# Odd rows of an eight-fold Fourier split: two residues in one tile, rows 376 apart summed and subtracted before the products

## The chip, the cores and the metric

The kernel runs on one core of a Trainium2 chip. A core has five engines with a queue each, which run their instructions in order and wait for one another through semaphores: TensorE (PE, matrix products; PEld is its weight load), VectorE (DVE), ScalarE (ACT), GpSimd (POOL) and SyncE (SP, which issues transfers). The metric is the device time of one execution in microseconds; all times here are in microseconds unless marked ns.

## The reference

```python
def _attn_ref(x):                      # x: (8, 3008, 256) float32
    X = np.fft.fft(x, axis=1)
    X = np.fft.fft(X, axis=2)
    return X.real.astype(np.float32)

def _moe_ref(x, w_in, w_out):          # x: (24064, 256), w_in: (256, 2048), w_out: (2048, 256)
    h = x @ w_in
    g = np.where(h > 0.0, h, 1.0 * (np.exp(np.minimum(h, 0.0)) - 1.0))
    return (g @ w_out).astype(np.float32)
```

The second function gets the result of the first, reshaped to 24064 rows of 256. So: a Fourier transform over 3008 rows and 256 channels for each of eight batches, real part, then two layers with an ELU between them.

## The kernel before, in words

**The main work.** The real part of the transform is symmetric, so half of the output rows (1504 a batch) give the rest. They are laid as columns, 256 to a tile, n_tiles = 47 tiles of 8 steps (376 steps). The transformed rows of a batch lie in two rings in SBUF (Rr for the cosine part, Ir for the sine part). One step i has, on PE, P (Wc times Rr, two products into a bank H), Q (Ws times Ir, two products added into the same bank), and for earlier steps seven products X1 (three), X2 (two) and X3 (two) into pA to pD. Between P and Q, DVE's E (even_part, L1263, two instructions) reads the bank, so Q waits for E. Then come h_minus (DVE, L1277), the ELU on ACT and DVE (g_plus and g_minus, L1293) and four sums and differences on POOL (sum_1, sum_3, sum_2, sum_4, in this order; L548), from which the seven products save an eighth. X1's third product reads what sum_2 writes, X2 what sum_3 and sum_1 write, X3 what sum_4 writes.

**How the order is set.** Every action is put into a list with a planned time, and the list is sorted and emitted; all that goes through `pin` keeps that order on its engine. A step is T = 4.8 long in the plan. Within a step: P at 0.0, E at 0.9, Q at 2.17, h_minus at 3.55; on POOL sum_4 of step i-2 at 0.3, then sum_1, sum_3, sum_2 of step i-1 at 2.91, 3.6 and 4.4. X1 of step i-2 stands at 0.87, behind P and ahead of Q; in the first step of a tile's eight X3 of the step before is moved behind P as well. At the end of a tile, in steps that are 1 modulo 8, comb_1 and comb_2 (two DVE instructions) stand at 4.2 and 4.21; comb_22 and comb_3 follow one step later at 1.0 and 2.5, the transposes turn_u and turn_v two and three steps later at 4.2, and each transpose is followed by SP's output transfers. Transfers of SP are not pinned, and run earlier than planned where they can.

**The transform.** Batches 2 to 7 (the Quarter class) split the 1504 half rows by eight. For the batch b, steps are counted from r0 = 48b - 70 by `rel`, so that r0 is 2 modulo 8:

- load_quarter (L276) brings four tiles j = 0 to 3 of x, first near rows (96 partitions) and then far rows (94 partitions); a partition holds four rows of 256, the residues m = 0 to 3 of a row number modulo 8. Two of the four (rows in rising order) come by SP (L301), two (falling order) by one indirect transfer each on POOL (L288). On POOL these are j = 1 in step 2, j = 2 in step 3 (5 for b = 2), j = 0 in step 27 and j = 3 in step 28, all at 1.3.
- mirror_sum (POOL), half_sum (DVE) and channel_fold (POOL) fold rows and channels into tiles e and o. quarter_pairs in steps 43 to 53 pairs them: for kodd = 0 on POOL, for kodd = 1 on DVE with multipliers of a table (L815, two instructions a call, at 4.25).
- at_quarter runs four transforms (ri = 0, 1 and kodd = 0, 1). Each has an even half and an odd half of four products into a bank H, in steps 51, 56, 59 and 64 and two steps later, at 4.75. The odd half (L963 to L967) has products of 189 or 188 columns: residues 1 and 3, u and v.
- DVE then spreads the halves, and join writes the rings: in steps 54, 59, 75 and 76.

A product in float32 shows in the trace as two PE passes with a weight load each, so counts of PE instructions are twice the counts of products.

The odd half before, and the place of the pairs for kodd = 1:

```python
            c, m = (378, 189) if self.kodd else (379, 188)
            yield (u, 1), c, 189, 0
            yield (u, 3), c + 189, 189, 0
            yield (v, 1), c + 378, m, 189
            yield (v, 3), c + 378 + m, m, 189
```
```python
        for n, step in enumerate((43, 44, 45, 46, 51, 53)):
            ri, m = divmod(n, 3)
            rel(step, 4.25, quarter_pairs, b, ri, 1, (2, 1, 3)[m])
```

Of the kernel before, what the change touches and what calls it, by code (L numbers as in the profile page):

```python
# [28 lines left out]
BE = 4 * NH  # L29
BW = BE + 3 * NE  # L30
NA = (95, 94)
QW = (1133, 1134)
GW = 7 * TW
PERIOD = 4.8
BS = 4
# [37 lines left out]
    return out.reshape(128, -1).astype(np.float32)  # L73


def _quarter_consts():

    p = np.arange(96)[:, None]

    def rows(m):  # L80
        s = 8 * p + m if m < 4 else 8 * (93 - p) + m
        return s, (p < (95 if m == 0 else 94)).astype(np.float64)

    out = []
    for ri in range(2):
        fn = np.cos if ri == 0 else np.sin
        for kodd in range(2):

            def block(m, k):
                s, w = rows(m)  # L90
                w = np.where(s == 0, 0.5, w)
                w = np.where(s == RUN, 0.5 if ri == kodd else 0.0, w)
                return w * fn(2.0 * np.pi * ((s * k[None, :]) % SEQ) / SEQ)

            def twist(m, n):
                s, w = rows(m)
                a = np.arange(n)[None, :]
                phi = np.pi * s / HALF
                turn = 2.0 * np.pi * ((2 * a * s) % HALF) / HALF
                c, d = np.cos(phi), np.sin(phi)  # L100
                if ri:
                    return w * d * np.cos(turn), w * c * np.sin(turn)
                return w * c * np.cos(turn), -w * d * np.sin(turn)

            n = 94 if kodd else 95
            near = 2 * np.arange(n) + kodd
            a, b = block(0, near), block(4, near)
            if kodd:
                (u1, v1), (u3, v3) = twist(1, 189), twist(3, 189)
                u2, v2 = twist(2, 95)  # L110
                parts = [a, u2, b, v2, u1, u3, v1, v3]
            else:
                ev, od = 4 * np.arange(189), 4 * np.arange(188) + 2
                parts = [a, b, block(2, ev[:95]), block(2, od[:94])]
                parts += [block(1, ev), block(3, ev), block(1, od), block(3, od)]
            out += parts
    return np.concatenate(out, axis=1).astype(np.float32)


def _turn_consts():  # L120
    p = np.arange(96)
    out = []
    for m in (1, 3, 2):
        t = np.tan(np.pi * np.minimum(8 * p + m, RUN - 1) / HALF)
        out += [t, -1.0 / t, 1.0 / t, -t]
    return np.stack(out, axis=1).astype(np.float32)


# [34 lines left out]
def kernel(  # L163
# [112 lines left out]
    def load_quarter(b, j, far):  # L276

        L = spool.tile([128, 6 * ND], FP, tag=f"xl{j}", bufs=1, name=f"xq{j}")
        if j == 0:
            state["rest"] = L[:, 4 * ND :]  # L280
        state["L", j, far] = L = L[:, 0 : 4 * ND]
        back = j in (1, 2)
        base = (0, SEQ, HALF, HALF)[j]
        if back != far:
            n = 94 if far else 96
            c = 3 if far else 5 if j == 1 and b == NB - 1 else 4
            pin(
                nc.gpsimd.indirect_dma_start(  # L288
                    out=L[0:n],
                    out_offset=None,  # L290
                    in_=xflat,
                    in_offset=bass.IndirectOffsetOnAxis(
                        ap=ix[0:n, c : c + 1].bitcast(U32), axis=0
                    ),
                    element_offset=(b * SEQ + (HALF if j in (1, 3) else 0)) * ND,
                )
            )
            return
        row = base - 751 if far else base
        for p, q in ((0, 80), (80, 94)) if far else ((0, 96),):  # L300
            nc.sync.dma_start(out=L[p:q], in_=xrows(b, row + 8 * p, 8, q - p, 4))  # L301

    CC = cpool.tile([128, 384], FP, tag="CC")
    w2 = cpool.tile([128, NF * ND], FP, tag="w2")
# [205 lines left out]
            out=t[0:96, 0 : QW[kodd]], in_=QM_dr.ap()[:, n : n + QW[kodd]]  # L510
        )

    twist_tab = cpool.tile([128, 12], FP, tag="turns")

    warm = cpool.tile([128, 1], FP, tag="warm")
    nc.vector.memset(warm, 0.0)
# [220 lines left out]
    def mirror_sum(j, far, m):  # L737

        n = 94 if far else 96
        own, other = lines(j, far)[0:n], lines((1, 2)[j == 3], far)[0:n, ::-1]  # L740
        gtt(own[:, m, 1:], own[:, m, 1:], other[:, m, :0:-1], ALU.add)
        if m == 0:
            gtt(own[:, :, 0:1], own[:, :, 0:1], other[:, :, 0:1], ALU.add)

    def half_sum(kodd, far, h):
# [32 lines left out]
    def quarter_row(b):  # L778

        L = state["L", 1, 0]  # L780
        if b == NB - 1:
            for i in range(3):
                act(L[0:1, i * ND : i * ND + ND], L[0:1, i * ND + ND : i * ND + 2 * ND])
        act(L[0:1, 3 * ND :], state["L", 0, 0][0:1, 0:ND])

    def quarter_pairs(b, ri, kodd, m):

        near, far = state["F", ri, kodd]
        slot = lambda m: (near, far)[m // 4][0:94, 128 * (m % 4) : 128 * (m % 4) + 128]
        parts = state.setdefault(("Q", ri, kodd, b), {0: near[0:95, 0:128], 4: slot(4)})  # L790
        if not kodd:
            if m == 1:
                state["pairs"] = spool.tile(
                    [128, 384], FP, tag="side", bufs=2, name="pairs"
                )
            new = state["pairs"]
            a, z = (
                t[0:94, 128:512].rearrange("p (m d) -> p m d", d=128)
                for t in (near, far)
            )  # L800
            o = new[0:94].rearrange("p (m d) -> p m d", d=128)
            if m == 1:
                gtt(o, a, z[:, ::-1], ALU.add)
            else:
                gtt(z[:, ::-1], a, z[:, ::-1], ALU.subtract)
            for k in (1, 2, 3):
                parts["u", k] = new[0:94, 128 * k - 128 : 128 * k]
                parts["v", k] = slot(8 - k)
            return
        new = (near, near, far)[m - 1][0:94, (512, 640, 512)[m - 1] :]  # L810
        parts["u", m], parts["v", m] = new[:, 0:128], slot(8 - m)
        for i, o in ((0, parts["u", m]), (1, parts["v", m])):
            c = 4 * (0, 2, 1)[m - 1] + 2 * ri + i
            pin(
                nc.vector.scalar_tensor_tensor(  # L815
                    out=o, in0=parts["v", m], scalar=twist_tab[0:94, c : c + 1],
                    in1=slot(m), op0=ALU.mult, op1=ALU.add,
                )
            )

    def fold_first(L):

# [125 lines left out]
    class Quarter(Dft):  # L948
        def parts(self, par):

            u, v = ("v", "u") if self.ri and not self.kodd else ("u", "v")
            if not par:
                order = (
                    ((0, 94), (("u", 2), 95), (4, 94), (("v", 2), 95))
                    if self.kodd
                    else ((0, 95), (4, 95), ((u, 2), 95), ((v, 2), 94))
                )
                c = o = 0
                for key, n in order:
                    yield key, c, n, o  # L960
                    c, o = c + n, o + n
                return
            c, m = (378, 189) if self.kodd else (379, 188)  # L963
            yield (u, 1), c, 189, 0
            yield (u, 3), c + 189, 189, 0
            yield (v, 1), c + 378, m, 189
            yield (v, 3), c + 378 + m, m, 189  # L967

        def mms(self, par, ps):
            parts = list(self.parts(par))  # L970
            for j, (key, c, n, o) in enumerate(parts):
                w = self.stat[key]
                K = w.shape[0]
                mm(
                    ps[:, o : o + n],
                    w,
                    QM[self.ri, self.kodd][0:K, c : c + n],
                    j == 0,
                    j == len(parts) - 1,
                )  # L980
            if par:
                self.odd = ps
            else:
                self.even = ps
# [932 lines left out]
    for b in range(2, NB):  # L1917
# [3 lines left out]
        def rel(step, dt, fn, *key):  # L1921
            at((r0 + step) * T + dt, lambda: fn(*key))
# [7 lines left out]
        rel(5, 3.0, quarter_row, b)  # L1930
        for far, start in ((0, 6), (1, 30)):
            for n in range(8):
                rel(start + n, 1.3, mirror_sum, (0, 3)[n % 2], far, n // 2)
        for step, *key in (
            (13, 0, 0, 0), (20, 1, 0, 0), (21, 0, 0, 1), (22, 1, 0, 1),
            (35, 0, 1, 0), (36, 1, 1, 0), (37, 1, 1, 1), (38, 0, 1, 1),
# [14 lines left out]
        for n, step in enumerate((43, 44, 45, 46, 51, 53)):  # L1951
            ri, m = divmod(n, 3)
            rel(step, 4.25, quarter_pairs, b, ri, 1, (2, 1, 3)[m])
        for step, ri, kodd, finish, join in (
            (51, 0, 0, 0, 54),
            (56, 1, 0, 0, 59),
            (59, 0, 1, 60, 75),
            (64, 1, 1, 66, 76),
        ):
            at_quarter(r0 + step, b, ri, kodd, r0 + finish, r0 + join)  # L1960
# [52 lines left out]
```

## Time and profile before

| | |
|---|---|
| median of 3 runs | 1916.73 us (1916.56 to 1917.5) |
| the profiled execution | 1918.8 us; its span, first to last instruction, 1917.0 |
| granted TensorE clock | 1.0 throughout |
| PE, DVE, ACT, POOL busy | 99%, 75%, 46%, 70% of the span |
| POOL sums (L548, G<-G) | 1440, 736 ns each |
| indirect loads (L288) | 24, 0.91 to 1.50 each |
| L815 pairs on DVE | 72, of 0.35 or 0.77 |
| loads by SP (L301) | 36 issues, 0.34 each in the median |
| SP waits for the transposed output (L1494 <- L1441) | 733.7 |

The page gives busy times and groups of instructions. A group's row has engine, operation, what it writes and reads, count, busy time, mean ns of one, and the idle time of the engine before it with what ended it. The timeline has one row for instructions of a kind that follow each other: start, length, engine, line, operation, operands and count; in brackets the idle time before it and what ended that. A row with x4 is four instructions. A wait is put down to the one that came last.

### The profile page before, as it was taken

What the parts mean: (1) busy time and instruction counts of PE and PEld (TensorE: products, weight loads), DVE (VectorE), ACT (ScalarE), POOL (GpSimd) and SP (SyncE); (2) the same over time, 40 slices, a digit from 0 to 9 for tenths busy, and PEclk for the clock granted to TensorE, in tenths of its full rate; (3) what the DMA queues carried; (4) which work ended last, traced back from release to release, by engine and by line L of the source; (5) the groups of instructions that cost most, each with busy time, mean ns of one, the idle gap of its engine ahead of it and who ended that gap; (6) DMA issues with size and microseconds to landing.
All of it is one profiled execution on the core that took longest, in us unless ns stands there. A gap on an engine that the chain in (4) does not pass through costs nothing.

```text
span 1917.0 us, 27564 instructions
## 1 busy us (share of the span) xinstructions
PE 1906.6 (99%) x8972; PEld 1656.8 (86%) x8972; DVE 1430.8 (75%) x2714; ACT 877.5 (46%) x1712; POOL 1348.7 (70%) x1837
## 2 busy tenths in 40 slices
PE   9999999999999999999999999999999999999999
PEld 6888888888888888888888888888888888888887
DVE  8766667877778777777777777777777777667666
ACT  5754444444444444444444444444444444344443
POOL 3888668776677766777667776687766876556565
PEclk9999999999999999999999999999999999999999
DMA  8146212111011110211101111022110210100101
GB/s 338 45 33 44 54 30 54 39 22 33 12 44 36 32 29 12 51 31 29 27 19 45 34 28 26 12 52 44 24 20 12 54 21 15 17 12 14 20 12 23
DMA packets 271072, 71.88 MB, mean 37 GB/s; under 512 B 256814, under 2 KB 257730, under 8 KB 270928
## 3 DMA queue, kind: packets, MB, share of 16 engines
q1 hardware_dynamic: 257296, 57.34, 15.1%
q0 software_dynamic: 11456, 12.52, 2.2%
q8 instruction: 71, 1.16, 0.2%
q14 instruction: 73, 0.60, 0.1%
q10 hardware_dynamic: 2176, 0.26, 0.1%
HBM read 45.20 MB, written 24.80 MB: 37 GB/s over the span
## 4 chain that ended last, share of the span: by engine, by line
PE 96%; DVE 2%; DMA 1%; ACT 1%; issue 0%; POOL 0%; SPq 0%; DVEq 0%; POOLq 0%
PE H L539 38%; PE pB L539 17%; PE pC L539 17%; PE pD L539 17%; PE pA L539 9%; DMA raw<-in_moe_w_in_dram 0%; DVE e L636 0%; DVE pow L407 0%; DVE E L1263 0%; POOL w L548 0%; DVE o L636 0%; ACT Wsc L551 0%; ACT G L551 0%; ACT M L551 0%; DMA wex<-wx 0%
## 5 line engine op out<-in xcount | busy, mean ns | idle before, releaser
L548 POOL TENSOR_TENSOR G<-G 128x256 f32<-128x256 f32 x1440 | 1046.2, 736 | 513.3 <-DVE G L1293 353.1
L551 ACT ACTIVATE G<-H 128x512 f32<-128x512 f32 x376 | 224.5, 597 | 930.9 <-DVE G L1277 927.2
L1263 DVE SCALAR_TENSOR_TENSOR E<-Rb,wex,H 128x256 f32<-128x256 f32 x752 | 328.1, 478 | 374.4 <-PE H L539 367.6
L539 PE MATMUL H<-Ir,Wsc 128*128 128x256 f32 x1504 | 386.7, 380 | 1.4 <-DVE E L1263 1.4
L539 PE MATMUL H<-Rr,Wsc 128*128 128x256 f32 x1504 | 387.3, 380 | 0.5 <-ACT Wsc L551 0.5
L539 PE MATMUL pC<-G,WT 128*128 128x256 f32 x1440 | 369.5, 379 | 0.0
L539 PEld LDWEIGHTS H<-Ir,Wsc 128*128 128x128 f32 x1504 | 278.4, 189 | 49.2 <-DVE E L1263 3.8
L539 PEld LDWEIGHTS H<-Rr,Wsc 128*128 128x128 f32 x1504 | 282.5, 190 | 41.7 <-issue 2.3
L539 PEld LDWEIGHTS pC<-G,WT 128*128 128x128 f32 x1440 | 273.6, 190 | 37.2
L1277 DVE SCALAR_TENSOR_TENSOR G<-E,H 128x512 f32<-128x512 f32 x376 | 257.2, 684 | 46.6 <-POOL G L548 13.2
L1293 DVE SCALAR_TENSOR_TENSOR G<-G,H 128x512 f32<-128x512 f32 x376 | 256.1, 681 | 40.7 <-ACT G L551 40.6
L1293 DVE SCALAR_TENSOR_TENSOR G<-M,G 128x512 f32<-128x512 f32 x376 | 257.1, 684 | 0.7 <-ACT M L551 0.7
L551 ACT ACTIVATE G<-G 128x512 f32<-128x512 f32 x376 | 233.4, 621 | 0.0
L539 PE MATMUL pB<-G,w 128*128 128x256 f32 x784 | 229.3, 379 | 0.0
L539 PE MATMUL pA<-G,w 128*128 128x256 f32 x784 | 229.3, 379 | 0.0
L539 PE MATMUL pD<-G,w 128*128 128x256 f32 x784 | 229.3, 379 | 0.0
L551 ACT ACTIVATE M<-G 128x512 f32<-128x512 f32 x376 | 224.3, 596 | 2.8 <-DVE G L1277 2.8
L551 ACT ACTIVATE M<-M 128x512 f32<-128x512 f32 x376 | 221.1, 588 | 0.1
L539 PE MATMUL pB<-G,WT 128*128 128x256 f32 x720 | 214.3, 379 | 0.0
L539 PE MATMUL pD<-G,WT 128*128 128x256 f32 x720 | 214.1, 379 | 0.0
L539 PEld LDWEIGHTS pA<-G,w 128*128 128x128 f32 x784 | 148.9, 190 | 20.5
L539 PEld LDWEIGHTS pB<-G,w 128*128 128x128 f32 x784 | 148.9, 190 | 20.4 <-PE H L539 0.2
(170 smaller groups left out, 1529.8 us busy)
## 6 DMA issues: line engine op xcount, KB each, us to landing
out_dram<-ot SPq DMA_DIRECT2D x496, 32.0 KB
xq<-in_x_dram SPq DMA_DIRECT2D x12, 384.0 KB
out_dram<-ot SPq DMA_DIRECT2D x256, 2.0 KB
xq<-in_x_dram SPq DMA_DIRECT2D x12, 320.0 KB
Rb<-r SPq DMA_DIRECT2D x10, 376.0 KB
raw<-in_moe_w_in_dram SPq DMA_DIRECT2D x7, 512.0 KB
MC<-dft_mats SPq DMA_DIRECT2D x3, 943.5 KB
xl<-in_x_dram SPq DMA_DIRECT2D x4, 512.0 KB
```

What stands on the lines that cost most here:

```text
L539: nc.tensor.matmul(out_, lhsT=lhsT, rhs=rhs, start=start, stop=stop, skip_group_check=True)
L548: pin(nc.gpsimd.tensor_tensor(out=o, in0=a, in1=b, op=op))
L551: pin(nc.scalar.activation(out=o, in_=i, func=func, **kw))
L1263: nc.vector.scalar_tensor_tensor(out=S.E[:, c], in0=Rb[:, cols(i)], scalar=wex[:, f : f + 1], in1=S.H[:, c], op0=ALU.mult, op1=ALU.add,)
L1277: nc.vector.scalar_tensor_tensor(out=two(S.G[:, 0:512])[:, :, ::-1], in0=two(S.E), scalar=2.0, in1=two(S.H), op0=ALU.mult, op1=ALU.subtract,)
L1293: nc.vector.scalar_tensor_tensor(out=o, in0=e, scalar=-1.0, in1=h, op0=ALU.add, op1=ALU.max)
```

## The change

Residues 1 and 3 of the odd rows are no longer held side by side. Rows 376 apart (SHIFT = 8 x 47) are put into two tiles at the same partition: 47 partitions with rows 8p + 3, 47 with rows 8p + 1, and the rows 376 higher in the other place. After the pairs, a new function shift_pairs forms the sum and the difference of the two; the sum goes with the even wave numbers and the difference with the odd ones, so each product has half the columns, written to every second column of the bank. For kodd = 1 this holds for all four products of the odd half, for kodd = 0 for two of four. It takes other load patterns, other constants and another order of the mirror sums. The diff, cut to what the text speaks of:

```diff
-QW = (1133, 1134)
+QW = (944, 756)
+NP = 47
+SHIFT = 8 * NP
...
         if back != far:
             n = 94 if far else 96
-            c = 3 if far else 5 if j == 1 and b == NB - 1 else 4
-            pin(
-                nc.gpsimd.indirect_dma_start(
-                    out=L[0:n],
...
+            for i in (0, 2) if far else (3, 1):
+                c = 3 if far else 5 if j == 1 and b == NB - 1 and i == 3 else 4
+                pin(
+                    nc.gpsimd.indirect_dma_start(
+                        out=rows[0:n, i],
...
+            row = base + (749 if far else -3)
+            for i, shift in (((3, 0), (1, SHIFT)) if far else ((2, 0), (0, SHIFT))):
+                nc.sync.dma_start(
+                    out=rows[0 : 2 * NP, i],
...
+                        ap=[[2 * ND, 2], [-8 * ND, NP], [1, ND]],
...
+            if not far:
+                nc.sync.dma_start(
+                    out=rows[2 * NP : 96, 0::2][:, 0:2],
...
             return
-        row = base - 751 if far else base
-        for p, q in ((0, 80), (80, 94)) if far else ((0, 96),):
-            nc.sync.dma_start(out=L[p:q], in_=xrows(b, row + 8 * p, 8, q - p, 4))
+
+        def ahead(p, n, first, row, step):
+            nc.sync.dma_start(
+                out=rows[p : p + n, first::2][:, 0:2],
...
+        for p, n in ((0, 80), (80, 14)) if far else ((0, 96),):
+            ahead(p, n, int(far), base + 8 * p - 750 * far, 2)
+        for p, m, n in ((0, 3, NP), (NP, 1, NP if far else 96 - NP)):
+            ahead(p, n, int(not far), base + m - 752 * far, SHIFT)
...
-        if m == 0:
+        if m == 1:
             gtt(own[:, :, 0:1], own[:, :, 0:1], other[:, :, 0:1], ALU.add)
...
         L = state["L", 1, 0]
-        if b == NB - 1:
-            for i in range(3):
-                act(L[0:1, i * ND : i * ND + ND], L[0:1, i * ND + ND : i * ND + 2 * ND])
...
-        parts["u", m], parts["v", m] = new[:, 0:128], slot(8 - m)
+        parts["u", m], parts["v", m] = new[:, 0:128], slot(1 if m == 1 else 8 - m)
         for i, o in ((0, parts["u", m]), (1, parts["v", m])):
...
+            turn(o, slot(8 - m), 4 * (0, 2, 1)[m - 1] + 2 * ri + i, slot(m), ALU.add)
+
+    def turn(o, a, c, b, op):
+
+        pin(
+            nc.vector.scalar_tensor_tensor(
+                out=o, in0=a, scalar=twist_tab[0:94, c : c + 1],
+                in1=b, op0=ALU.mult, op1=op,
+            )
+        )
+
+    def shift_pairs(b, ri, kodd, k):
+
+        near = state["F", ri, kodd][0][0:94]
+        parts = state["Q", ri, kodd, b]
+        m = "uv".index(k)
+        low, high = parts[k, 1], parts[k, 3]
+        sign = ALU.add, ALU.subtract
+        if kodd:
+            new = near[:, (384, 256)[m] :][:, 0:128], low
+            for o, f in zip(new, sign):
+                turn(o, high, 12 + (ri != m), low, f)
+        else:
+            new = near[:, 128:256], near[:, 384:512]
+            for o, f in zip(new, sign):
+                vtt(o, low, high, f)
+        for i in range(2):
+            parts[k, "+-"[i]] = new[i]
...
-            c, m = (378, 189) if self.kodd else (379, 188)
-            yield (u, 1), c, 189, 0
-            yield (u, 3), c + 189, 189, 0
-            yield (v, 1), c + 378, m, 189
-            yield (v, 3), c + 378 + m, m, 189
+            c = 378 if self.kodd else 379
+            for k, o in ((u, 0), (v, 189)) if self.kodd else ((u, 0),):
+                yield (k, "+"), c, 95, slice(o, o + 189, 2)
+                yield (k, "-"), c + 95, 94, slice(o + 1, o + 188, 2)
+                c += 189
+            if not self.kodd:
+                yield (v, 1), c, 188, slice(189, 377)
+                yield (v, 3), c + 188, 188, slice(189, 377)
...
-                rel(start + n, 1.3, mirror_sum, (0, 3)[n % 2], far, n // 2)
+                rel(start + n, 1.3, mirror_sum, (0, 3)[n % 2], far, (0, 2, 1, 3)[n // 2])
...
             rel(step, 4.25, quarter_pairs, b, ri, 1, (2, 1, 3)[m])
+        for step, *key in (
+            (47, 0, 1, "u"), (48, 0, 0, "u"), (49, 0, 1, "v"), (50, 1, 0, "v"),
+            (54, 1, 1, "u"), (55, 1, 1, "v"),
+        ):
+            rel(step, 4.25, shift_pairs, b, *key)
```

## The prediction

> **What bounds the kernel now.** I read the page first, then the timeline of TensorE (PE), VectorE (DVE) and GpSimd (POOL) around one batch (b=3), then the waits. Steps are counted from r0 of the batch, as in the code: E of step 27 starts at 552.90, of step 47 at 647.89, of step 54 at 683.31. On the page PE is busy for the whole span, and the chain that ended last lies on PE for 96%:
>
> ```profile
> PE 1906.6 (99%) x8972; PEld 1656.8 (86%) x8972; DVE 1430.8 (75%) x2714; ACT 877.5 (46%) x1712; POOL 1348.7 (70%) x1837
> ```
>
> So PE is the bound, at a period of 4.75 us a step (11 products of 256 columns, 0.43 each), and two things count: columns taken from PE, and any stall put into it. The averages of DVE and POOL say that there is room; the timeline says where there is none.
>
> **What PE saves.** The timeline of PE, at an even half (four products of 94 or 95 columns) and an odd half (four of 188 or 189) of one transform:
>
> ```profile
> 670.57 0.36 PE L539 MATMUL H<-QM,e 95*128 95x95 f32 x2
> 670.76 0.39 PE L539 MATMUL H<-QM,o 94*128 94x95 f32 x2
> 670.99 0.39 PE L539 MATMUL H<-QM,pairs 94*128 94x95 f32 x2
> 671.21 0.39 PE L539 MATMUL H<-QM,o 94*128 94x94 f32 x2
> 671.43 1.06 PE L539 MATMUL H<-Rr,Wsc 128*128 128x256 f32 x4
> ...
> 680.96 0.81 PE L539 MATMUL H<-QM,pairs 94*128 94x189 f32 x4
> 681.60 0.80 PE L539 MATMUL H<-QM,o 94*128 94x188 f32 x4
> 682.25 1.03 PE L539 MATMUL H<-Rr,Wsc 128*128 128x256 f32 x4
> ```
>
> From start to start a 95-column product takes 0.22 (670.76 to 670.99; two passes), a 189-column one 0.32 ((682.25 - 680.96)/4). Halving the columns saves 0.10, not half. With kodd=1 all four products of the odd half shrink (1.29 to 0.88, saves 0.41), with kodd=0 two (saves 0.20). Two of each a batch: 1.23 us; six batches: **-7.4**. The outputs are now written with a step of two columns, which no row shows. From one side: no cost, as 95 columns need 0.16 at the full rate (95 x 0.43/256) of the 0.22; from the other, a half-rate write would make 95 columns as long as 189, and the saving goes (0), or doubles the 0.22 (+2.6 a batch at worst). I take no cost: the nearest row is the contiguous 95-column one.
>
> **What DVE adds.** shift_pairs is 12 instructions a batch (six calls of two), 94x128 with both inputs in SBUF. The nearest row is L815, same shape, same place in a step; DVE and POOL beside each other:
>
> ```profile
> 631.72 0.35 DVE L815 SCALAR_TENSOR_TENSOR e<-o,twist_tab,e 94x128 f32<-94x128 f32 x1
> 632.10 0.77 DVE L815 SCALAR_TENSOR_TENSOR o<-o,twist_tab,e 94x128 f32<-94x128 f32 x1
> ```
> ```profile
> 631.20 0.72 POOL L548 TENSOR_TENSOR G<-G 128x256 f32<-128x256 f32 x1
> 632.00 0.73 POOL L548 TENSOR_TENSOR G<-G 128x256 f32<-128x256 f32 x1
> ```
>
> Each ends 0.15 after the POOL instruction that was running when it started (631.92 to 632.07, 632.73 to 632.87). So a pair lasts until the second POOL boundary after its start, plus 0.15. Now the six places. A call stands at 4.25 of its step, behind h_minus and, in steps 47 and 55, behind comb_1 and comb_2 too (47 + r0 is 1 modulo 8, where those stand at 4.2). Step 47, and the E of step 48 behind it:
>
> ```profile
> 651.06 0.68 DVE L545 TENSOR_TENSOR u<-p,pB 128x512 f32<-128x512 f32 x1
> 651.84 0.69 DVE L545 TENSOR_TENSOR v<-u,pC 128x512 f32<-128x512 f32 x1
> 652.64 0.87 DVE L1263 SCALAR_TENSOR_TENSOR E<-Rb,wex,H 128x256 f32<-128x256 f32 x2
> ```
> ```profile
> 652.39 0.73 POOL L548 TENSOR_TENSOR G<-G 128x256 f32<-128x256 f32 x1
> 653.08 0.99 POOL L548 TENSOR_TENSOR pairs<-e,o 94x384 f32<-94x384 f32 x1
> ```
>
> Behind E waits PE's Q: its weight load starts at 653.57, 0.06 after E's end (653.51), and in most steps the weight load of H<-Ir shows the same 0.07 of waiting for E. In step 29, where E came 0.10 late, PE lost about 0.03. So the cushion is 0.07 and the rest is paid one to one.
> - Step 47: first of the pair starts about 652.5, ends 653.12 + 0.15; second ends 654.07 + 0.15 = 654.22. E starts 0.08 before that (instructions overlap so), at 654.14 instead of 652.64: PE loses 1.50 - 0.07 = **1.43**.
> - Step 48: no loss by a hair. E of 49 has PE's X3 and X1 ahead of Q (Q at 658.48, E's end at 657.40, 1.08 spare), and the new pair brings it about 0.9 late. Steps 49 and 50 (turn_u, turn_v): E had 1.2 idle before it, the pair takes about 1.1: nothing. A margin missed costs 0.1 to 0.3 each.
> - Step 54: pair starts 687.0; POOL boundaries at 687.44 and 688.25, so it ends 688.40; E at 688.32 instead of 688.06: **0.18**.
> - Step 55: as 47. Pair from 692.61, POOL boundaries 693.29 and 693.97, end 694.12; E at 694.04 instead of 692.81, both sides 0.18 later: **1.16**.
>
> Sum 2.77 a batch, six batches: **+16.6**. If POOL did not hold it up a pair would take 0.7 (2 x 0.35), E would be 0.55 late at 47 and 55, and the sum is 2 x 0.48 x 6 = 5.8: the lower bound. Missed margins make 3.5 a batch, 21, the upper.
>
> **What POOL adds.** Each of the four indirect loads a batch becomes two. In steps 27 and 28 (j=0 and j=3, 94 rows):
>
> ```profile
> 552.97 1.49 POOL L288 DMA_INDIRECT xq<-in_x_dram,ix  x1 [0.18 <-issue]
> 554.52 3.46 POOL L548 TENSOR_TENSOR G<-G 128x256 f32<-128x256 f32 x4
> 558.16 1.49 POOL L288 DMA_INDIRECT xq<-in_x_dram,ix  x1 [0.18 <-issue]
> 559.68 3.48 POOL L548 TENSOR_TENSOR G<-G 128x256 f32<-128x256 f32 x4
> ```
>
> POOL has no idle time there: sums, load, sums. The load stands ahead of sum_1, and PE's third X1 product (pB<-G,WT) needs sum_2, the third of the four. In step 28 sum_2 ends at 562.06 and that weight load starts at 562.84: 0.78 spare. Two more loads at 1.49 + 0.18 push it 3.34 later: PE loses 2.56, 0.46 in step 28's X1 and the rest one step on. The sums there are stretched by DVE's join (0.88 and 1.03 instead of 0.73), and partly slide out of it: I take 2.3. Six batches: **+13.8**. The new loads have a quarter of the bytes per row, which no row shows at 94 rows; from the one side, the 96-row loads of steps 2 and 3 take 0.92 + 0.15, and with that price PE would lose about 0.1 a batch (0.6 in all); from the other, the loads that open the program stand 0.3 apart, 1.80 each: 2.8 a batch, 17. The first eight indirect loads (L239) have rows of 4 KB and 2 KB in turn and take 0.94 to 1.24 with no order by size, so I keep 1.49.
>
> [...]
>
> In steps 2 and 3 (96 rows) POOL idles 0.68 and 0.65 before its sums, so two times 1.07 leave it 0.8 late, against 1.5 of spare before X1: nothing; without that cover 2.1 a batch.
>
> **Costed at nothing.** SP issues 24 loads a batch instead of 6 (L301: 36 in all), 18 x 0.34 = 6 us, under 734 us in which SP waits for the transposed output; were that cover gone, stores would hold the two output tiles and DVE's transposes. The reordered mirror sums only swap rows; half_sum(35) now follows its last mirror sum in the same step, with some 2 us between (0.9 a batch if not). ACT loses three 0.4 us copies in the last batch, ACT is at 46%. Landing of the 94-row loads takes 11 to 12 us (96 rows 4.0); their first reader comes 14 us after: covered, and the pieces are smaller.
>
> **Sum.** -7.4 + 16.6 + 13.8 = +23.0. The profiled execution took 1918.8 (span 1917.0 and 1.8 around it), so a profiled one would take 1941.8; the median of the runs shown is 1916.7, 2.1 below, so **1939.7**.
>
> **Rivals.**
> - Faster: the added DVE and POOL work falls into idle time (25% and 30% on average). -7.4 gives 1909. It decides if the stalls stay under 1.23 us a batch; the only place that could do it is E of steps 48 and 56, and there DVE has 0.1 idle. 0.07.
> - Same, within 0.2% (3.8 us, about what a measurement of this kernel can tell from no change): pairs at 0.7 and POOL at the 96-row price: -7.4 + 5.8 + 0.6 = 1916. 0.06.
> - POOL's price is by bytes, only DVE stalls: -7.4 + 16.6 + 0.6 = 1926.5. For it: quarter rows; against: L239. 0.15.
> - DVE's pair escapes POOL, only POOL stalls: -7.4 + 5.8 + 13.8 = 1929. Against: every L815 pair. 0.07.
> - The change does not do what it says (stepped outputs eat PE's saving) or the hair margins of steps 48 to 50 break: +3 to +12 more, 1943 to 1952. 0.12.
> - The forecast, 1931 to 1946: 0.53.
>
> **Chances and range.** Faster 0.07, same 0.06, slower 0.87. The range leaves out the first two rivals and little above: 1922 to 1950.
>
> **What would show it.** Weight loads H<-Ir waiting for DVE E about 1.4, 0.2 and 1.2 in steps 48, 55, 56 of each batch; weight loads pB<-G,WT waiting for POOL G 0.5 and 1.8 in steps 28 and 29; 48 indirect loads with a mean near 1.2; odd halves of 0.88 and 1.09 from first product to the next P; PE busy down by some 7 and idle by some 30. The prediction is wrong if PE shows no such gaps, if a 94-row quarter load takes 0.9, or if 95-column products with stepped outputs stand more than 0.22 apart.

## The result, and the profile after

The changed kernel took 1942.25 us in the median of four runs (1941.26, 1941.78, 1942.72 and, profiled, 1948.1), the kernel before 1916.69 on the same chip: ratio 1.0139, 95% interval 1.0118 to 1.0159. It is slower by 25.6, where +23.0 was forecast. The profiled execution is 6 above the others; the prediction has nothing for that, and why is part of what follows.

The page of the changed kernel, its busy times and the chain that ended last (lines of the helpers have moved: matmul L587, POOL's sums L596, E L1332):

```profile
PE 1909.4 (98%) x8972; PEld 1649.0 (85%) x8972; DVE 1468.0 (75%) x2786; ACT 876.5 (45%) x1709; POOL 1380.8 (71%) x1861
...
PE 86%; DVE 5%; POOL 4%; DMA 2%; issue 1%; SPq 1%; ACT 0%; DVEq 0%; POOLq 0%
```

PE runs as many instructions as before, and is busy for 1909.4 instead of 1906.6. Its share of the chain fell from 96% to 86%: DVE, POOL, DMA and SP's queue now hold pieces of it. The waits of the changed kernel (who waits, for whom, us in total, times, longest) say where:

```profile
PEld H L587 <- DVE E L1332: 21.2, 24, 1.6
...
PEld pB L587 <- POOL G L596: 16.8, 15, 1.9
...
POOL xs L596 <- DMA xs<-xe_dr: 7.5, 1, 7.5
PEld H L587 <- POOL xe L596: 5.7, 1, 5.7
```

Before, the first was 3.8 in 7 waits and the second 0.6 in 2; the other two were not there. So there are three kinds of stall. I take the size of each from PE's own starts: the time from one pass to the next, less the 0.22 of a pass without a wait.

**Kind 1, E behind a pair.** DVE, POOL and PE at steps 47 and 48 of b=3 (start, length, operation, count, idle before it):

```profile
664.63 1.82 DVE L863 SCALAR_TENSOR_TENSOR e<-o,twist_tab,e 94x128 f32<-94x128 f32 x2
666.38 0.86 DVE L1332 SCALAR_TENSOR_TENSOR E<-Rb,wex,H 128x256 f32<-128x256 f32 x2
```
```profile
664.58 0.73 POOL L596 TENSOR_TENSOR G<-G 128x256 f32<-128x256 f32 x1
665.27 1.04 POOL L596 TENSOR_TENSOR pairs<-e,o 94x384 f32<-94x384 f32 x1
```
```profile
667.29 1.13 PE L587 MATMUL H<-Ir,Wsc 128*128 128x256 f32 x4 [1.21 <-DVE E L1332]
```

The pair ends at 666.45, 0.14 after POOL's second instruction (666.31), and E comes after it. PE's starts lose 1.47 to 1.48 here in every batch, 0.19 to 0.32 at step 55 and 0.88 to 1.02 at step 56 (0.67 in the last batch).

**Kind 2, X1 behind the loads.** POOL and the weight loads in step 28 of the same batch:

```profile
569.57 1.49 POOL L303 DMA_INDIRECT xq<-in_x_dram,ix  x1 [0.18 <-DVE G L1362]
571.37 1.50 POOL L303 DMA_INDIRECT xq<-in_x_dram,ix  x1 [0.30 <-issue]
572.89 5.20 POOL L596 TENSOR_TENSOR G<-G 128x256 f32<-128x256 f32 x7
```
```profile
568.63 0.30 PEld L587 LDWEIGHTS pB<-G,WT 128*128 128x128 f32 x2 [0.71 <-POOL G L596]
```

A quarter of the bytes, and still 1.49 for each load; the second has 0.30 of idle before it, where 0.18 stands before the first. PE loses 0.50 to 0.72 in step 28 and 1.76 to 1.78 a step later.

**Kind 3, once, at 198 us.** SP and POOL of the changed kernel, where the short rows (xs, one channel of all batches) are loaded:

```profile
188.78 0.30 SPq L1180 DMA_DIRECT2D xe_dr<-x  x1
189.12 0.70 SPq L337 DMA_DIRECT2D xq<-in_x_dram  x2
190.42 0.39 SPq L1186 DMA_DIRECT2D xs<-xe_dr  x1
190.85 2.91 SPq L1190 DMA_DIRECT2D xs<-xe_dr  x1
193.80 3.73 SPq L337 DMA_DIRECT2D xq<-in_x_dram  x4
```
```profile
197.16 0.39 POOL L596 TENSOR_TENSOR xs<-xs 128x96 f32<-128x96 f32 x1 [7.47 <-DMA xs<-xe_dr]
```

Before, SP issued the last of these xs loads at 182.56 and POOL went on at 189.4. Now five of batch 2's near loads (L317, L326, L337) stand ahead of the last xs load in SP's order, where one stood. Their issues take 2.7 in all, the one took 0.35. The last xs load is issued at 190.85, POOL waits 7.47, and PE loses 5.44. The other 6 of the 8.3 lie in SP's issues and waits that were there before and took longer in this execution, such as 9.68 instead of 7.42 for the four loads of x at 170.82.

The wait costs more than its length. These are the short rows' products behind it, in the changed kernel and in the kernel before, and the row of the changed kernel for the stretch 197.71 to 201.11 (its length, the busy times of PE, PEld, DVE, ACT and POOL, then the granted clock):

```profile
197.96 3.74 PE L587 MATMUL H<-MC,xe 128*8 128x189 f32 x24 [5.28 <-POOL xe L596]
```
```profile
193.60 2.09 PE L539 MATMUL H<-MC,xe 128*8 128x189 f32 x24
```
```profile
197.71:201.11 3.40, 3.15 (x23) 1.55 (x24) 0.00 (x0) 0.00 (x0) 3.24 (x7) 0.50 0.39 107
```

The granted clock is 0.50 there, and the same 24 passes take 1.65 more. So kind 3 costs 5.44 + 1.65 = 7.1.

**PE's saving.** The odd halves of the transforms, PE of the changed kernel, first kodd = 0, then kodd = 1:

```profile
694.68 0.58 PE L587 MATMUL H<-QM,e 94*128 94x95 f32 x4
695.10 0.83 PE L587 MATMUL H<-QM,o 94*128 94x188 f32 x4
695.77 1.03 PE L587 MATMUL H<-Rr,Wsc 128*128 128x256 f32 x4
...
737.85 1.03 PE L587 MATMUL H<-QM,e 94*128 94x95 f32 x8
738.71 1.06 PE L587 MATMUL H<-Rr,Wsc 128*128 128x256 f32 x4
```

From the first product to the next P: 1.09 and 0.86, both 1.29 before. Eight passes in 0.86 are 0.108 each, 0.215 a product: the stepped output costs nothing.

So the sum of this execution is -7.4 + 30.3 (5.0 a batch) + 7.1 = +30.0 by the predicted saving, and 1948.1 - 1918.8 = 29.3 by the two profiled executions. The 0.7 between them lies at the start: PE's first pass of P stands at 27.81 in the profile after and at 28.48 in the one before. In the profiles of the runs below it stands at 25.81 to 26.70, so both of these executions also began late, by 1.5 and 2.1 against a middle of 26.3.

### The profile page after: what moved, and what is told of

Read it like the earlier page. It is cut to its first block, busy times and chain, and to the rows that moved or that the text cites. A ratio compares the mean times of both kernels' runs of the same rounds, so it can differ in the third digit from the quotient of the medians.

```text
span 1946.3 us, 27882 instructions
## 1 busy us (share of the span) xinstructions
PE 1909.4 (98%) x8972; PEld 1649.0 (85%) x8972; DVE 1468.0 (75%) x2786; ACT 876.5 (45%) x1709; POOL 1380.8 (71%) x1861
## 3 DMA queue, kind: packets, MB, share of 16 engines
q8 instruction: 71, 1.16, 0.3%
## 4 chain that ended last, share of the span: by engine, by line
PE 86%; DVE 5%; POOL 4%; DMA 2%; issue 1%; SPq 1%; ACT 0%; DVEq 0%; POOLq 0%
PE H L587 34%; PE pB L587 15%; PE pC L587 15%; PE pD L587 15%; PE pA L587 8%; POOL G L596 2%; DMA x<-in_x_dram 2%; POOL xq L303 2%; DVE e L863 1%; DVE E L1332 1%; DVE v L593 1%; DVE G L1362 1%; DVE G L1346 0%; DVE u L593 0%; SPq L1162 0%
## 5 line engine op out<-in xcount | busy, mean ns | idle before, releaser
L596 POOL TENSOR_TENSOR G<-G 128x256 f32<-128x256 f32 x1440 | 1047.8, 737 | 497.5 <-DVE G L1362 344.0
L1332 DVE SCALAR_TENSOR_TENSOR E<-Rb,wex,H 128x256 f32<-128x256 f32 x752 | 327.4, 476 | 356.6 <-PE H L587 351.6
L587 PE MATMUL H<-Ir,Wsc 128*128 128x256 f32 x1504 | 388.8, 381 | 12.3 <-DVE E L1332 12.2
L587 PE MATMUL H<-Rr,Wsc 128*128 128x256 f32 x1504 | 387.6, 380 | 0.5 <-ACT Wsc L599 0.5
L587 PE MATMUL pC<-G,WT 128*128 128x256 f32 x1440 | 369.6, 379 | 0.0
L587 PEld LDWEIGHTS H<-Ir,Wsc 128*128 128x128 f32 x1504 | 277.8, 189 | 65.2 <-DVE E L1332 21.2
L587 PEld LDWEIGHTS H<-Rr,Wsc 128*128 128x128 f32 x1504 | 282.1, 190 | 41.8 <-issue 1.7
L587 PEld LDWEIGHTS pC<-G,WT 128*128 128x128 f32 x1440 | 273.6, 190 | 37.2
L1346 DVE SCALAR_TENSOR_TENSOR G<-E,H 128x512 f32<-128x512 f32 x376 | 257.0, 683 | 58.6 <-POOL G L596 24.6
L587 PE MATMUL pB<-G,w 128*128 128x256 f32 x784 | 229.3, 379 | 0.0
L587 PE MATMUL pA<-G,w 128*128 128x256 f32 x784 | 229.3, 379 | 0.0
L587 PE MATMUL pD<-G,w 128*128 128x256 f32 x784 | 229.3, 379 | 0.0
L587 PE MATMUL pB<-G,WT 128*128 128x256 f32 x720 | 215.7, 381 | 11.2 <-POOL G L596 11.2
L599 ACT ACTIVATE M<-G 128x512 f32<-128x512 f32 x376 | 223.9, 596 | 2.8 <-DVE G L1346 2.8
L587 PE MATMUL pD<-G,WT 128*128 128x256 f32 x720 | 214.2, 379 | 0.0
L587 PEld LDWEIGHTS pA<-G,w 128*128 128x128 f32 x784 | 149.0, 190 | 20.5
L587 PEld LDWEIGHTS pB<-G,w 128*128 128x128 f32 x784 | 148.9, 190 | 20.4 <-PE H L587 0.2
```

Source lines behind the costliest of these rows:

```text
L587: nc.tensor.matmul(out_, lhsT=lhsT, rhs=rhs, start=start, stop=stop, skip_group_check=True)
L596: pin(nc.gpsimd.tensor_tensor(out=o, in0=a, in1=b, op=op))
L599: pin(nc.scalar.activation(out=o, in_=i, func=func, **kw))
L1332: nc.vector.scalar_tensor_tensor(out=S.E[:, c], in0=Rb[:, cols(i)], scalar=wex[:, f : f + 1], in1=S.H[:, c], op0=ALU.mult, op1=ALU.add,)
L1346: nc.vector.scalar_tensor_tensor(out=two(S.G[:, 0:512])[:, :, ::-1], in0=two(S.E), scalar=2.0, in1=two(S.H), op0=ALU.mult, op1=ALU.subtract,)
```

## The experiments

The theory: three kinds of stall, each with its own cause, take back more than PE saves, and the saving itself is whole. Rivals: POOL's price goes by bytes; the stepped outputs cost PE time; the spread between runs has nothing to do with SP's order. Numbers of the runs are those of their labels (run 8, an earlier form of run 10, gave no result). The kernel before was timed beside each group of runs: 1916.6 to 1916.8.

### 1. The loads alone

The kernel before, with each indirect load of a row of four cut into two halves of 2 KB:

```diff
+            for h in range(2):
-                    out=L[0:n],
+                        out=L[0:n, 2 * ND * h : 2 * ND * h + 2 * ND],
-                    element_offset=(b * SEQ + (HALF if j in (1, 3) else 0)) * ND,
+                            b * SEQ + (HALF if j in (1, 3) else 0) + 2 * h
```

> The kernel before, each of its 24 indirect loads cut into two of half the columns (2 KB a row), all else unchanged. Theory: an indirect load costs POOL a fixed 1.5 us (94 rows) or 0.9 (96 rows) and 0.3 ahead of it, whatever its bytes, so PE waits for sum_2 in steps 28 and 29 of each batch, about 2.4 us a batch: +14.5, about 1931, with weight loads pB<-G,WT waiting for POOL. Rival, price by bytes: each half takes about half, no wait, 1917.

Measured 1930.65 (1930.34 to 1931.33), ratio 1.0067 (1.0044 to 1.009): +14.1. PE lost 0.49 to 0.72 and 1.76 to 1.78 a batch at X1, and nothing at E. The loads took 1.49 to 1.50 with half the bytes of a row, as with the whole row before and a quarter of it after. So the price does not go by bytes, and kind 2 comes from the number of loads alone.

### 2. The pairs alone

The kernel before, with the same 72 DVE instructions in the same places, of the same shape, written to columns that nothing reads; the products stay as they were:

```diff
+        for step, *key in (
+            (47, 0, 1, "u"), (48, 0, 0, "u"), (49, 0, 1, "v"), (50, 1, 0, "v"),
+            (54, 1, 1, "u"), (55, 1, 1, "v"),
+        ):
+            rel(step, 4.25, shift_pairs, b, *key)
```

> The kernel before with the 72 instructions of shift_pairs at their places, same operands and sizes, their results written to columns that nothing reads (one constant column for the multiplier); products and loads as before. Theory: E of steps 48, 55 and 56 comes late and PE's Q waits 1.5, 0.1 to 0.2 and 1.0 a batch: +15.8, about 1932.5. Rival, the pairs escape POOL or fit into idle time (0.35 each): +5.8 or less, at most 1922.5. Rival, that they only delay because POOL is late from its loads: 1917.

Measured 1932.18 (1932.04 to 1932.29), ratio 1.0075 (1.0051 to 1.0098): +15.6, with 1.46 to 1.48, 0.19 to 0.33 and 0.67 to 1.01 a batch. Kinds 1 and 2 add up: 14.1 + 15.6 - 7.4 = +22.3. The changed kernel's fastest run is at +24.6, so something over 2 is missing even there.

### 3. The pairs elsewhere

The changed kernel, the pairs at other steps and mostly ahead of h_minus (3.5 in a step) instead of behind it:

```diff
-            (47, 0, 1, "u"), (48, 0, 0, "u"), (49, 0, 1, "v"), (50, 1, 0, "v"),
-            (54, 1, 1, "u"), (55, 1, 1, "v"),
+            (48, 3.5, 0, 1, "u"), (49, 3.5, 0, 0, "u"), (50, 3.5, 0, 1, "v"),
+            (51, 4.26, 1, 0, "v"), (53, 4.26, 1, 1, "u"), (56, 3.5, 1, 1, "v"),
```

> The changed kernel with the six calls of shift_pairs at other places: ahead of h_minus in steps 48, 49, 50 and 56, behind h_minus in steps 51 and 53, where E has over 1 us of idle time ahead of it. Theory: the waits of Q for E go nearly all (2.6 a batch), POOL's stay: 15 below the changed kernel, about 1927. Rival, the DVE work is too much wherever it stands: no change, 1942.

Measured 1928.68 (1926.24 to 1930.85), ratio 1.006 (1.004 to 1.008). Kind 2 stayed as it was. At E 0.26 a batch was left, in step 50, where the pair of step 49 and the transpose turn_u stand in one step, and single stalls of 0.98 in two batches. Kind 3 cost nothing in this profile, with the same order on SP: the last xs load was issued at 182.7. So most of kind 1 is a matter of place.

### 4. 96 rows instead of 94

The changed kernel, far loads of 96 rows with the row numbers shifted so that all stay inside the batch; nothing reads the two added rows:

```diff
-            (3, 128, 748),
+            (3, 128, 764),
-            n = 94 if far else 96
+            n = 96
-                            b * SEQ + (HALF if j in (1, 3) else 0) + i
+                            b * SEQ + (HALF if j in (1, 3) else 0) + i - 16 * far
```

> The changed kernel, its 24 indirect far loads with 96 rows instead of 94 (two more rows of x into partitions that nothing reads). Theory: what makes a load cost POOL 1.5 instead of 0.9 is the 94 rows, so the loads take 0.92, step 28 has no wait and step 29 at most 0.5: 12 to 14 below the changed kernel, about 1929. Rival, the 1.5 comes from the place (DVE beside it) or the far rows' addresses: still 1.5, 1942.

Measured 1935.94 (1930.82, 1933.12, 1938.76, 1940.41), ratio 1.0102 (1.0073 to 1.0131), so the gain was there, but less than expected and with a wide spread. POOL in step 28 of b=3, in the profile of the 1930.82 run:

```profile
558.46 0.92 POOL L303 DMA_INDIRECT xq<-in_x_dram,ix  x1
559.68 0.92 POOL L303 DMA_INDIRECT xq<-in_x_dram,ix  x1 [0.30 <-issue]
560.62 5.70 POOL L596 TENSOR_TENSOR G<-G 128x256 f32<-128x256 f32 x7
```

More rows, and 0.92 instead of 1.49. The stall at X1 fell from 2.3 or 2.5 to between 0.6 and 1.1 in five batches and 1.6 in the last. It did not go, because two loads of 0.92 with 0.15 and 0.30 of idle take 2.3 of a step, where the one load of before took 1.67. This profile has no stall of kind 3 either (last xs load at 180.9), and the other three executions, up to 1940.41, have no profile.

### 5. Both together

> The changed kernel with the edits of the third and the fourth run together. The terms add: 1916.6 of before, -7.4 of shorter products, 3.9 of stalls at E that the third run kept (0.26 in each batch and two or three single ones), 5 of stalls behind the sums that the fourth run kept (0.6 to 1.1 a batch): 1918, plus a stall of 0 to 6 before step 26 where POOL waits for the last loads of the short rows. Rival, the two kinds of stall hide each other (a late sum gives DVE a boundary less): under 1914. Rival, a term was left out that the fourth run's median of 1935.9 showed: over 1926 in the median with no front stall in the profile.

Measured 1921.61 (1919.34 to 1925.59), ratio 1.0024 (1.0015 to 1.0034); the profiled execution was the one of 1919.34 and has no stall of kind 3. What it lost to the batches' stalls, some 9.5, gives 1916.7 - 7.4 + 9.5 = 1918.8: the terms add in that execution, and neither rival holds. The median lies 2.3 above it; no profile shows why.

### 6. The xs loads first

The changed kernel; `pin` holds an engine's instructions in the planned order, here for the xs loads and batch 2's near loads on SP:

```diff
+    def first_pin(b):
+        return pin if b == 2 else lambda i: i
...
-                nc.sync.dma_start(
+                first_pin(b)(nc.sync.dma_start(
                     out=rows[0 : 2 * NP, i],
...
-                nc.sync.dma_start(
+                pin(nc.sync.dma_start(
                     out=xs[:, j, :, 0:4],
```

> The changed kernel, with the last loads of the short rows (xs) and the near loads of batch 2 kept in the planned order on SP, so that the new loads come behind them. Theory, the new SP loads of batch 2 stand between those loads and make POOL's fold late, by an amount that differs from run to run: the last xs load is issued by 183, POOL's fold waits under 2, PE has no gap over 0.5 before the stall at step 28 of batch 2, and all runs lie within 1.5 of one another at 1938.5 to 1940.5 (1916.6 - 7.4 + 30.3 = 1939.5). Rival, the spread has another cause: median 1941 to 1943 and runs up to 1948 again.

Measured 1946.03 (1944.87 to 1948.37), ratio 1.015 (1.0132 to 1.0168): slower than the changed kernel, and outside both theories. The last xs load was issued at 179.2, POOL went on at 188.1, and PE's stall at 198 was gone, as expected. But there was a new one of 5.2 in all from 218 on: a wait of 4.0, and slower passes behind it, as the granted clock was 0.50 from 219.5 to 222.8. SP and POOL of this run:

```profile
196.97 1.99 SPq L329 DMA_DIRECT2D xq<-in_x_dram  x1
199.07 13.48 SPq L1566 DMA_DIRECT2D out_dram<-ot  x24
212.59 1.63 SPq L340 DMA_DIRECT2D xq<-in_x_dram  x3
```
```profile
215.19 0.72 POOL L599 TENSOR_TENSOR xq<-xq,xq 96x255 f32<-96x255 f32 x1 [6.64 <-DMA xq<-in_x_dram]
```

The near loads of tile 3, planned one step later, now stood behind 24 output stores on SP, and the mirror sum on POOL waited for them. Without that stall this execution would be at 1944.87 - 5.2 = 1939.7, where theory wanted 1939.5. So here SP's order made the stall: runs 6 and 7 have it, and runs 9 and 11, which issue these loads ahead of the 24 stores, do not. For the stall at 198 the same is argued, not shown. It is gone in the four profiles with the xs loads kept together (runs 6, 7, 9 and 11), but runs 3, 4 and 5 keep the changed kernel's order on SP there and lost nothing either, with the last xs load at 182.7, 180.9 and 183.5, and run 10, with it at 184.4, had PE wait 0.73. The new loads took as long in run 3 as in the changed kernel's profile, 2.7. What differed is how long SP's other issues took, and no run shows why. That the spread of the changed kernel's runs comes from kind 3 is not shown either.

### 7. All three mended, first try

Run 5, with run 6's order, one far load in each of steps 27 to 30, and the pairs moved once more:

```diff
+            if far:
+                fetch(0)
+                state["later", j] = lambda: fetch(2)
...
+        for j, n in ((0, 29), (3, 30)):
+            rel(n, 1.3, lambda j: state["later", j](), j)
...
+            (48, 3.5, 0, 0, "u"), (50, 3.5, 0, 1, "u"), (52, 3.5, 1, 0, "v"),
+            (53, 4.26, 1, 1, "u"), (54, 3.5, 0, 1, "v"), (56, 3.5, 1, 1, "v"),
```

> The changed kernel with 96-row far loads, one in each of steps 27 to 30, the pairs of shift_pairs in steps 48, 50, 52, 53, 54 and 56 at other places, and the short rows' loads first. Theory, the saving on PE is the whole 7.4 and all that was lost are the three kinds of stall: 1909 to 1912, PE with no gap over 0.5 in batches 2 to 7. Rival, the stepped outputs cost part of the saving, or loads in four steps only spread POOL's stall: 1913 or more, with products of 95 columns in the odd halves over 0.22 apart or gaps at X1 in steps 28 to 31.

Measured 1924.18 (1922.12 to 1927.64), ratio 1.0034 (1.0021 to 1.0048). Kind 2 was gone (no gap at X1 of steps 28 to 31), so one load a step is hidden. Lost were 7.9 at 220, which is run 6's stall at the tile 3 loads (a wait of 5.8, and a granted clock of 0.50 up to 223.9), and some 1.2 a batch at E of steps 54 and 56: two pairs in a row in step 53, and in step 54 a pair that made h_minus and all that follows it late. Without the stall at 220 the profiled execution (1924.65) would be at 1916.8.

### 9. All three, second try

```diff
-            (0, ((0, 2, 0.2), (1, 2, 1.3), (3, 3, 0.2), ...
+            (0, ((0, 2, 0.2), (1, 2, 1.3), (3, 2, 1.4) if b == 2 else (3, 3, 0.2), ...
-            (53, 4.26, 1, 1, "u"), (54, 3.5, 0, 1, "v"), (56, 3.5, 1, 1, "v"),
+            (56, 3.5, 0, 1, "v"), (60, 3.5, 1, 1, "u"), (61, 3.5, 1, 1, "v"),
```

> As the seventh run, but with the near loads of tile 3 of batch 2 ahead of the output stores on SP (step 2 instead of 3), and the pairs in steps 48, 50, 52, 56, 60 and 61. In the seventh run's profile 7.8 went to one stall at 220 where POOL waited for loads that stood behind 32 stores on SP, and 1.2 a batch to E of steps 54 and 56. Theory, nothing else is lost: 1909 to 1911.5, no gap over 0.3 in batches 2 to 7 and none over 0.6 before. Rival, the pairs find a POOL boundary to wait for wherever they stand: 0.5 to 1 a batch at E of steps 61 and 62, 1912.5 to 1916. Rival, the first stall moves once more: 1913 or more with one gap over 2 between 195 and 230.

Measured 1916.12 (1914.57 to 1918.15), ratio 0.9996 (0.9987 to 1.0005): in its profile (the execution of 1917.76) there is no kind 3 at all and no kind 2, and the rival for the pairs came: 0.64 a batch at one place and 0.85 at another in four of six. The second, DVE and POOL of b=2:

```profile
425.70 2.58 DVE L873 SCALAR_TENSOR_TENSOR e<-o,twist_tab,e 94x128 f32<-94x128 f32 x2
428.20 0.67 DVE L1356 SCALAR_TENSOR_TENSOR G<-E,H 128x512 f32<-128x512 f32 x1
```
```profile
425.76 0.92 POOL L306 DMA_INDIRECT xq<-in_x_dram,ix  x1 [0.30 <-issue]
426.69 3.04 POOL L606 TENSOR_TENSOR G<-G 128x256 f32<-128x256 f32 x4
```

The second instruction of the pair started during a load (426.11) and lasted 2.17, over the load's end and two sums. A pair that stands ahead of the E of the next step pays for all of that.

### 10. What a load's rows cost

Run 4's kernel with two more loads a batch into unread columns:

```diff
+                for h, k in enumerate(
+                    ((80, 88), (64, 92), (48, 90), (32, 95), (16, 72), (94, 96))[b - 2]
+                ):
```

> The fourth run's kernel with two more indirect loads a batch, behind those of tile 3, of 80 and 88, 64 and 92, 48 and 90, 32 and 95, 16 and 72, 94 and 96 rows in batches 2 to 7, written to columns that nothing reads; only the length of each on POOL is read. Theory, a load is short when its rows are a multiple of 16: 80, 64, 48, 32, 16, 96 at or under 0.93, and 88, 92, 90, 95, 72, 94 near 1.5. Rival, only multiples of 32 are short: 80, 48 and 16 near 1.5 too. Rival, multiples of 8 are short: 88 and 72 at or under 0.93. Rival, the price grows with the rows: 0.15 for 16 rows to 0.92 for 96. The time by 2 x 1.3 of POOL work in step 28: 3 to 10 more than the fourth run.

The time, one run, was 1951.55, more than the 3 to 10 over run 4 that was expected. Some 8 of it are the clock, by an estimate from kind 3, where 3.4 at 0.50 cost 1.65: behind four of the five longest waits of PE for the sums behind the loads the granted clock was 0.50 for 16.6 in all, in 568.1 to 571.4, 1052.8 to 1056.1, 1295.2 to 1298.5 and 1537.5 to 1544.2, and the passes there took longer. Here is the last batch, 94 and then 96 rows, on POOL:

```profile
1533.21 1.66 POOL L321 DMA_INDIRECT xq<-in_x_dram,ix  x1 [0.30 <-issue]
1535.17 0.92 POOL L321 DMA_INDIRECT xq<-in_x_dram,ix  x1 [0.30 <-issue]
```

| rows | 16 | 32 | 48 | 64 | 80 | 96 | 72 | 88 | 90 | 95 | 92 | 94 |
|---|---|---|---|---|---|---|---|---|---|---|---|---|
| us on POOL | 0.89 | 0.89 | 0.90 | 0.93 | 1.02 | 0.92 | 0.96 | 0.99 | 0.96 | 1.14 | 1.21 | 1.66 |

The theory was half wrong: 72, 88 and 90 rows are no multiples of 16 and are short. None of the rivals fits either. Nine of the counts take 0.89 to 1.02, in no clear order (80 rows are the longest of them): six that 16 divides, then 72 (which 12 divides), 88 (11) and 90 (15). The three that none of these divides took 1.14 (95 rows, 5 x 19), 1.21 (92, 4 x 23) and 1.66 (94, 2 x 47). Each count but 96 and 94 was timed once, and no run shows what the divisors have to do with it.

### 11. The pairs where POOL idles

Run 9 with the pairs at 1.2 of a step: behind E and ahead of the ELU's two DVE instructions.

```diff
-            (48, 3.5, 0, 0, "u"), (50, 3.5, 0, 1, "u"), (52, 3.5, 1, 0, "v"),
-            (56, 3.5, 0, 1, "v"), (60, 3.5, 1, 1, "u"), (61, 3.5, 1, 1, "v"),
+            (53, 1.2, 0, 0, "u"), (55, 1.2, 1, 0, "v"), (58, 1.2, 0, 1, "u"),
+            (61, 1.2, 0, 1, "v"), (64, 1.2, 1, 1, "u"), (66, 1.2, 1, 1, "v"),
```

> As the ninth run, but the six pairs stand at 1.2 of steps 53, 55, 58, 61, 64 and 66: behind E and ahead of the ELU's two DVE instructions, where DVE waits some 0.9 for ACT and POOL is idle or in a single mirror sum or load. Theory, a pair takes 0.7 to 0.75 where POOL is idle and up to 1.2 beside a single POOL instruction, so that E of the next step keeps its time and the saving of 7.4 stays: 1909 to 1911, no gap over 0.3 in batches 2 to 7. Rival, the pair makes the ELU late, its sums on POOL late and X1 or the next E late: 0.3 to 0.8 for each pair that stands beside a POOL instruction, 1912 to 1918. Rival, the stepped outputs eat a part of the saving: no gap and still 1912 or more.

Measured 1910.29 (1910.28 to 1912.45), ratio 0.9969 (0.9958 to 0.998): faster than both kernels. Its page, two of its waits, and DVE and POOL around one pair:

```profile
PE 1900.0 (100%) x8972; PEld 1649.9 (86%) x8972; DVE 1458.8 (76%) x2786; ACT 876.7 (46%) x1709; POOL 1367.7 (72%) x1861
```
```profile
PEld H L597 <- DVE E L1342: 4.9, 11, 1.1
```
```profile
674.55 0.55 DVE L603 TENSOR_TENSOR e<-pairs 94x128 f32<-94x128 f32 x2
675.03 0.67 DVE L1372 SCALAR_TENSOR_TENSOR G<-G,H 128x512 f32<-128x512 f32 x1
```
```profile
674.02 0.73 POOL L606 TENSOR_TENSOR G<-G 128x256 f32<-128x256 f32 x1
675.85 3.03 POOL L606 TENSOR_TENSOR G<-G 128x256 f32<-128x256 f32 x4 [1.09 <-DVE G L1372]
```

POOL is idle from 674.75 to 675.85, the pair takes 0.55, and the ELU behind it starts 0.48 after the pair did. No gap over 0.3 is left in batches 2 to 7, some 1.1 in all, so 1916.7 - 7.4 + 1.1 = 1910.4, where 1910.29 was measured. So PE's saving is whole and the stepped outputs are free. The pairs stand at another place of DVE's own order here as well, ahead of the ELU, and no run separates what that gives from what POOL's idle time gives.

## Why the prediction was right

By its own steps:

- **PE saves 7.4: right.** The odd halves went from 1.29 to 1.09 and 0.86 (0.88 was said), and run 11 keeps the saving in the total. One sign came out otherwise: PE's busy time was to fall by some 7 and rose by 2.8, though in run 11, without the waits, it fell by 6.6 (1900.0). Of the difference 1.65 is the slow clock behind the stall at 198; passes at a wait also count as longer (1.13 for the four behind the wait at 667.29, 1.03 for others). The rival that stepped outputs eat the saving was also bounded too low: its own worst case, 2.6 a batch, is 16 and not 12.
- **Pairs 16.6: right, a little high.** 1.43, 0.18 and 1.16 a batch were said; 1.48, 0.19 to 0.32 and 0.67 to 1.02 came, and run 2 measured 15.6 for all. The rule it rests on, that such an instruction ends 0.15 after the POOL instruction that ran at its start, holds for 114 of the 120 L863 instructions in the changed kernel's trace, all that started during one of POOL's tensor-tensor instructions (0.14 or 0.15). Of the other six, one found POOL idle and five started during an indirect load. The hair margins of steps 48 to 50 held: no gap over 0.1 there.
- **Loads 13.8: right, with some luck.** 0.46 and 1.84 a batch were said, 0.50 to 0.72 and 1.76 to 1.78 came, 14.1 in run 1. Inside the term two errors nearly cancel: the second load of each pair has 0.30 ahead of it and not 0.18, and the 0.26 taken off because the sums slide out of join's way was a guess that came out too small. The choice of 1.49 for a smaller load of 94 rows was the right one; the rival by bytes fell with run 1, where a load of half the bytes still took 1.49. But the reason given (L239's loads show no order by size) only excluded bytes; that the price goes with the count of rows (94 rows 1.49, 96 rows 0.92 in run 4) was not seen, and it would have shown the mend. Nor would that mend have brought the loss to 0.1 a batch, as the prediction has it for the 96-row price: run 4 lost 0.6 to 1.6.
- **SP "costed at nothing": the step that is not sound.** "18 x 0.34 = 6 us, under 734 us in which SP waits" counts how long SP is busy on average. It leaves out what stands behind the new loads in SP's order. In batch 2 they put 2.4 more ahead of the last xs load, for which POOL and then PE wait, and in the profiled execution, where SP's other issues took longer too, that place cost 7.1: a wait of 5.4, and 1.65 because the granted clock fell to 0.50 behind it, a cost that the prediction has nowhere. With the same order it cost nothing in runs 3, 4 and 5. The new issues were also not all 0.34, but up to 0.75 ahead of that xs load and up to 4.4 in later batches.

The total was forecast 2.6 too low. By the terms that runs 1 and 2 measured (14.1 and 15.6) it would have been 1939.0, so some 3 of the median are open. The profiled execution comes out: 1948.1 less 7.1 of kind 3 and less the 1.5 by which it began late is 1939.5. The other three, 1941.26 to 1942.72, have no profile. A late start or a smaller stall of kind 3 could each make the 2 to 3 that they lie above that; which it was stays open.

## What to carry to other kernels

In these runs more DVE instructions for half the columns on PE were a good trade only where they stood beside an idle POOL: the same pairs cost 15.6 beside POOL's sums (run 2) and about 1 where POOL waits (run 11). Cost a load on the engine that issues it by its count and its row count (here 94 rows against 96: 1.49 to 0.92), not by bytes, and look at what stands behind it in that engine's order. After a long wait of PE, look at the granted clock too: here it was 0.50 for 3.4 behind a wait of 5.4, which cost 7.1 in all. Averages of busy time hide all of this; the timeline of one step on the engines concerned shows it.

## What the runs showed of the hardware that was not expected

- An indirect load of 94 rows holds POOL for 1.48 to 1.66 and one of 96 rows for 0.91 to 0.96, with no order by the bytes of a row (1, 2 or 4 KB); one of 92 rows took 1.21 and one of 95 rows 1.14. A load straight after another has 0.30 or 0.31 of idle before it, one behind a sum 0.14 to 0.21.
- An L863 instruction on DVE (94x128, both inputs in SBUF) that started during one of POOL's tensor-tensor instructions ended 0.14 or 0.15 after it: 114 of 114 in the changed kernel's trace. During an indirect load it is otherwise. Of five that started in one in that trace, four ended some 0.3 after the load; in runs 7 and 9 ten ended before the load did, after 0.34 or 0.35. Twelve in the traces of the changed kernel and of runs 3, 7, 9 and 11 waited longer, for two or three POOL ends (up to 2.17); nine of them had started during an indirect load and did not end with it. No run here tells why.
- Behind PE's waits of 2.5 to 5.8 the granted clock was 0.50 for a stretch of some 3.4 or 6.8: seven of eight such waits, one in the changed kernel's profile, one each in those of runs 6 and 7 and four of five in run 10 (not behind one of 2.57). Behind the shorter waits, up to 2.16, it stayed at 1.00 until PE's last pass.
- SP's issues took up to 5.0 us of SP's time each (the new loads L337 0.34 in the median), and differed from one execution to the next with the same order: one load of x ahead of the xs loads of kind 3 took 4.66 in the changed kernel's profile, 3.35 in run 3's and 4.97 in run 10's.
